# One reordering and one re-layout of an attention, router and mixture-of-experts kernel

## The chip, the cores and the metric

The kernel runs on one core of a Trainium2 chip. The metric is the device time of one execution in microseconds (us). Three executions of the kernel before gave 1012.26, 1013.10 and 1013.12 us; the median is 1013.1 us.

## The reference, cut to what matters

Three stages follow one another. Everything is computed in float32 or better.

```python
# 1. chunked attention: batch 4, 8 heads, 768 positions, head size 64; chunks of 32 queries see
#    16 positions to the left, 8 to the right and 8 memory keys
scores = scale * q_c @ k_full.T ; a = softmax(scores) ; out_c = a @ v_full
x = out as (3072 tokens, 512)
# 2. router and experts: 8 experts, 512 -> 1024 -> 512, one expert for each token
logits = x @ w_gate + modality_bias[modality_id] ; e = argmax(logits)
gate_w = softmax(logits)[e]
y = gate_w * (relu(x @ w1[e]) @ w2[e])
# 3. a rational activation between two products, 512 -> 2048 -> 512
h = y @ w_in
g = (a0 + a1 h + a2 h^2 + a3 h^3) / (1 + |b0 h| + |b1| h^2 + 1e-6)
out = g @ w_out
```

## The kernel before, in words

All instructions are put on their engines' queues in the order of the program text; nothing is reordered by a planner. A framework adds the semaphores. An engine takes its queue in order, so a waiting instruction holds up all behind it on that engine.

**Attention** (lines 30 to 282) works on 24 tiles of 128 tokens in a pipeline. One pass `t` of the loop issues `scores(t)` and `softmax(t)`, the loads of tile t+4, `ptrans(t-1)` (four transposes of the probabilities, copied out by ScalarE), `xtrans(t-3)` (four transposes of the finished values), `exps(t)` and `pv(t-2)` (the product with the values, then sums, reciprocals and a product on VectorE, and the write of the values to DRAM). Every four tiles, `gate1` and `gate2` make router logits. `scores` writes one of the two halves of the PSUM tile `pa` (two banks in one tile), `pv` writes the two banks of `pb`.

**Router in two halves.** Tiles 0 to 15 are routed while attention still runs (`first`, `first_ranks`, then `first_places` in pass 22), which gives two early slots: 128 tokens each of the commonest expert, gathered from DRAM by GpSimd. The weights of that expert are loaded in pass 21. After the loop, the tail of attention (lines 268 to 282) is interleaved with the first products of early slot 0 (`mm1_0(0, kk)`: two float32 matmuls for each kk, which show as four records). `second` (line 519) then routes the other 8 tiles (`pick`, `rank`, `place`, the one-hot products at line 571 that list each slot's tokens), computes both early slots in plain float32 (`mm1_0`, `relu`, `prep_h0`, `mm2_0`), starts slot 2 (`mm1(EARLY, part)`), and makes the gate values: `terms` (a subtraction on VectorE, an exponential on ScalarE), `gates`, `gate_parts`, the wide product `bg` (line 605) and the 24 matmuls at line 616. The outputs of the two early slots and the split of `w2` into a rounded high part and a remainder (`split_hi` on ScalarE, `split_lo` on VectorE) end it.

**Experts** (`moe`, line 827): 24 slots follow. A slot has 24 products `mm1` (line 818) and 24 products `mm2` (line 746), all 128x128 by 128x512 of the rounded type `F32R`, with eight transposes of the hidden values and four of the next slot's tokens between them. `mm1` writes the two banks of `pb`, `mm2` the half `s % 2` of `pa`. A filler converts the third stage's weights beside it. In the last pass four tiles of rows for the third stage are transposed as well (line 863): two into pool tiles, two into the halves of `pb`.

**Third stage** (`moe2`, line 1020): 6 blocks of 512 tokens, each with 16 steps of 12 products `h` (lines 1052 to 1054) and 12 products `a` (lines 1109 to 1111), 2304 in all.

**Where the operands lie.** The allocator rounds each tile up to 32 bytes of a partition. Pools on the left side grow upwards behind the constants, pools on the right side are stacked downwards from the top, and the tiles of one pool follow one another. In the kernel before, the starts modulo 512 bytes are: `ident` 128; `xs`, `hs`, `xg`, `w2h`, `w2l`, `hhl` 416; `w1r`, `w1h`, `w1l`, `w2r` 480 (behind `ys`, 2080 bytes, and `e0`, 32 bytes); early `h0` 384; `wih`, `wil`, `yh`, `yl`, `wo` 192; `gh`, `gl` 256 (behind two tiles `yr` of 2080 bytes).

Of the kernel before, what the change touches and what calls it, by code (L numbers as in the profile page):

```python
# [46 lines left out]
def attention(nc, tc, ex, ident, q, k, v, wg_d, mod, mbias, pos_u, out_u, constants):  # L47
# [8 lines left out]
    with ExitStack() as ctx:  # L56
# [57 lines left out]
        def scores(t):  # L114
            qt, kt = qs[t % NB_IN], kz[t % NB_IN]
            sc = ex.pa[:, t % 2]
            for hp in range(HP):
                for c in range(TC):
                    x = c // 2 * KP + c % 2 * CH
                    nc.tensor.matmul(  # L120
                        sc[CH * c:CH * c + CH, hp * P:hp * P + P], lhsT=qt[:, hp, CH * c:CH * c + CH], rhs=kt[:, :, hp, x:x + 64],
                        start=True, stop=True,
                    )
            sc_t[t] = sc.rearrange("p (h k) -> p h k", k=64)
# [36 lines left out]
        def pv(t):  # L161
            s = pT_t.pop(t)
            w = vz[t % NB_IN]
            ps = ex.pb
            n = 2 * (D + 1)
# [61 lines left out]
        for t in range(NT):  # L227
# [42 lines left out]
        xtrans(NT - 3)  # L270
        ex.prep_x0(0)
        pv(NT - 1)
        ins.close()
        ex.open_w2(ctx)
        xtrans(NT - 2)
        ex.mm1_0(0, 0)
        xtrans(NT - 1)
        gate1(NT // GT - 1, 0, GT - 1)
        ex.mm1_0(0, 1)
        gate2(NT // GT - 1, 0, GT - 1)  # L280
        gate_last(NT - 1)
        rt.second()

# [8 lines left out]
class Router:  # L292
# [226 lines left out]
    def second(self):  # L519
# [3 lines left out]
        for f in self.pick(n, NT):  # L523
            f()
        ex.mm1_0(0, 2)
        ex.split_hi(ex.w1r, ex.w1h, 0)
        ex.mm1_0(0, 3)
        ps = self.rank(n, NT)
        ex.prep_x0(1)
        ex.relu(0)  # L530
        ex.mm1_0(1, 0, 1, 2, 3)
        rest = self.first_rest()
# [11 lines left out]
        for f in (  # L544
# [19 lines left out]
        ):  # L564
            f()
        for i in range(1, 4):
            ex.split_hi(ex.w1r, ex.w1h, i)
        for i in range(2):
            ex.split_lo(ex.w1r, ex.w1h, ex.w1l, i)
        for t in range(NT):  # L570
            nc.tensor.matmul(tb, lhsT=self.at1[:, :, t] if t < n else at2[:, :, t - n], rhs=bt[:, :, t], start=(t == 0), stop=(t == NT - 1))
        ex.prep_h0(0, 0)
        ex.prep_h0(0, 1)
# [9 lines left out]
        V.tensor_scalar(out=f[:, 1], in0=tb, scalar1=0.0, scalar2=-1.0, op0=ALU.is_gt, op1=ALU.mult)  # L583
        ex.relu(1)
        cnt = self.tp.tile([P, 32], F32, tag="t", name="cnt")
        ex.mm2_0(0, 0)
        nc.tensor.matmul(cnt, lhsT=self.ones, rhs=some, start=True, stop=True)
        self.slots(c, end, off, f, cnt)
        for i in range(2, 4):
            ex.split_lo(ex.w1r, ex.w1h, ex.w1l, i)  # L590
# [6 lines left out]
        for part in range(3):  # L597
            ex.mm1(EARLY, part)
            if part < 2:
                ex.prep_h0(1, part)  # L600
        for step in (*rest[2:], *self.terms(n, NT), *self.gates(n, NT), *self.gate_parts()):
            step()
# [18 lines left out]
        V.scalar_tensor_tensor(out=self.ex.gate_s, in0=gs[:, 1], scalar=1.0 / GP, in1=gs[:, 0], op0=ALU.mult, op1=ALU.add)  # L621
        ex.out(0)
        ex.out(1, ex.ys1)
        for i in range(4):
            ex.split_hi(ex.w2r, ex.w2h, i)
            ex.split_lo(ex.w2r, ex.w2h, ex.w2l, i)
        ex.load_w(EARLY, ex.w2r, ex.w2v)

# [27 lines left out]
class Experts:  # L656


    def __init__(self, nc, tc, ident, xd, yd, w1, w2, src_u, pos_u, out_u, gate_s, flags):
        self.nc, self.tc, self.ident = nc, tc, ident  # L660
        self.xd, self.yd, self.src_u, self.pos_u, self.out_u, self.gate_s, self.flags = xd, yd, src_u, pos_u, out_u, gate_s, flags
        self.w1v = w1.rearrange("e (p k) f -> (e p) (k f)", k=4)
        self.w2v = w2.rearrange("e (p j) d -> (e p) (j d)", j=8)
        self.hps, self.yps, self.hT = {}, {}, {}
        self.ctx = ExitStack()
        self.sp = self.ctx.enter_context(tc.tile_pool(name="shared", side="right", bufs=1))
        self.ps = self.ctx.enter_context(tc.tile_pool(name="shared_ps", side="right", bufs=4, space=PSUM))
        self.pa = self.ps.tile([P, 2, 512], F32, name="pa", bufs=1)
        self.pb = self.ps.tile([P, 2, 512], F32, name="pb", bufs=1)
        self.hs = self.sp.tile([P, 8, P], F32, name="hs")  # L670
        self.xs = [self.sp.tile([P, 2, 4, P], F32R, name=f"xs{i}") for i in range(2)]
        self.xg = [self.sp.tile([P, D_M], F32, name=f"xg{i}") for i in range(3)]
        self.ys = self.sp.tile([P, D_M + 1], F32, name="ys")
        self.e0 = self.sp.tile([1, 1], I32, name="e0")
        self.w1r = self.sp.tile([P, 4, 1024], F32, name="w1r")
        self.w1h = self.sp.tile([P, 4, 1024], F32R, name="w1h")
        self.w1l = self.sp.tile([P, 4, 1024], F32R, name="w1l")
        self.w2r = self.sp.tile([P, 4, 1024], F32, name="w2r")
        self.xT = {}
# [61 lines left out]
    def mm2(self, s, g):  # L741
        ps = self.pa[:, s % 2]
        for i, w in ((0, self.w2h), (1, self.w2h), (0, self.w2l)):
# [7 lines left out]
    def out(self, s, y=None):  # L751
        nc, y = self.nc, self.ys if y is None else y
        nc.gpsimd.tensor_copy(y[:, D_M:].bitcast(U32), self.out_u[:, s:s + 1])
        nc.scalar.activation(y[:, 0:D_M], self.pa[:, s % 2], func=AF.Copy, scale=self.gate_s[:, s:s + 1])
        nc.gpsimd.indirect_dma_start(
# [12 lines left out]
    def mm1_0(self, s, *kks):  # L768
        if 0 in kks:
            self.hps[s] = [(self.pa if s == 0 else self.pb)[:, i] for i in range(2)]  # L770
        for kk in kks:
# [12 lines left out]
    def mm2_0(self, s, g):  # L784
        for n in range(4 * g, 4 * g + 4):
            self.nc.tensor.matmul(  # L786
                self.pa[:, s % 2], lhsT=self.h0[g][:, n % 4], rhs=self.w2r[:, n // 2, (n % 2) * 512:(n % 2) * 512 + 512],
                start=(n == 0), stop=(n == 7),
            )
# [19 lines left out]
    def mm1(self, s, part):  # L809
        h, l = self.xT[s]  # L810
        w1h, w1l = self.w1h, self.w1l
        if part == 0:
            self.hps[s] = [(self.pa if s == 0 else self.pb)[:, i] for i in range(2)]
        ps = self.hps[s]
# [12 lines left out]
def moe(nc, tc, ex, filler, rows):  # L827
# [5 lines left out]
    for i in range(EARLY + 1, NM + 1):  # L833
# [27 lines left out]
        if i == NM:  # L861
            for t in range(4):
                ps = ex.ps.tile([P, 4, P], F32, tag="t", name="yps") if t < 2 else ex.pb[:, t - 2].rearrange("p (k n) -> p k n", k=4)
                rows.prep(t, w1r[:, t, 0:D_M + 1], ps, rows.h, rows.l)
# [148 lines left out]
def moe2(nc, tc, rows, wih, wil, wod, consts, out):  # L1013
    with ExitStack() as ctx:
# [145 lines left out]
def program(nc, tc, q, k, v, mod, wg_d, mbias, w1, w2, w_in, w_out, a, b, out):  # L1160
    with tc.manual_schedule(), ExitStack() as ctx:
        cp = ctx.enter_context(tc.tile_pool(name="const", bufs=1))
        dp = ctx.enter_context(tc.tile_pool(name="dram", bufs=1, space=bass.MemoryType.DRAM))
        ident = cp.tile([P, P], F32, name="ident")
        make_identity(nc, ident)
        nc.scalar.preload_act_table_set("natural_log_exp_and_others")
        src_u = cp.tile([P, NS], U32, name="src_u")
        pos_u = cp.tile([P, NS], U32, name="pos_u")
        out_u = cp.tile([P, NS], U32, name="out_u")
# [4 lines left out]
        ex = Experts(nc, tc, ident, xd, yd, w1, w2, src_u, pos_u, out_u, gate_s, flags)  # L1174
        consts = Constants(nc, cp)
# [62 lines left out]
```

## Time and profile before

| what | value |
|---|---|
| runs | 1012.26, 1013.10, 1013.12 us |
| the profiled execution | 1014.01 us, span of its instructions 1012.2 us |
| TensorE matmuls (PE) | 975.7 us busy, 96% of the span |
| TensorE weight loads (PEld) | 780.8 us, 77% |
| VectorE (DVE) | 747.4 us, 74% |
| ScalarE (ACT) | 592.9 us, 59% |
| GpSimd (POOL) | 147.2 us, 15% |
| mean granted TensorE clock | 0.99 of full speed |

Attention takes the first 108 us or so, the second half of the router up to 157 us, the experts up to 463 us, the third stage the rest. A line of the timeline gives the start, the duration, the engine, the source line, what is written from what, the shape, the number of instructions merged into the line, and in brackets how long the engine was idle before it and what ended that. The 1.8 us between span and time lie before and behind the program's own instructions.

### The profile page before, as it was taken

The numbers are of one execution on the slowest core, as the hardware profiler recorded it, in microseconds if no ns is written. First come the engines' busy times: TensorE is split into PE (matmuls) and PEld (weight loads), VectorE is DVE, ScalarE is ACT, GpSimd is POOL, SyncE is SP. The second block draws the span as 40 slices with busy tenths as digits, with TensorE's granted clock in tenths as the row PEclk, the third lists the DMA queues.
The fourth block names the chain that finished last, engine by engine and source line by source line (L and its number), as shares of the span: only waits on it lengthen the run. The fifth ranks groups of instructions, "written<-read, shape, count | busy, mean of one in ns | idle before, by whom it ended". The sixth has DMA issues, their size and how long they took to land.

```text
span 1012.2 us, 16192 instructions
## 1 busy us (share of the span) xinstructions
PE 975.7 (96%) x5809; PEld 780.8 (77%) x5809; DVE 747.4 (74%) x1217; ACT 592.9 (59%) x947; POOL 147.2 (15%) x205
## 2 busy tenths in 40 slices
PE   6998989999999999989999999999999999999997
PEld 4776557888788888867888888888888888888885
DVE  6766555656685553345998988988888888889885
ACT  2543425555575554445766766776667676766673
POOL 5112012111143333220000100100010001001001
PEclk9999999999999999999999999999999999999999
DMA  8999422443696654345130100000010001001001
GB/s 261 377 363 350 178 74 74 123 128 107 203 311 224 234 152 127 114 147 218 65 112 15 42 11 22 31 21 21 22 43 11 22 11 42 21 1 42 1 1 42
DMA packets 37993, 110.43 MB, mean 109 GB/s; under 512 B 6950, under 2 KB 6978, under 8 KB 37892
## 3 DMA queue, kind: packets, MB, share of 16 engines
q1 hardware_dynamic: 27540, 76.43, 22.6%
q0 software_dynamic: 10352, 32.79, 9.2%
q8 instruction: 47, 0.77, 0.3%
q14 instruction: 54, 0.44, 0.1%
HBM read 82.44 MB, written 27.80 MB: 109 GB/s over the span
## 4 chain that ended last, share of the span: by engine, by line
PE 86%; DMA 6%; DVE 3%; issue 3%; ACT 2%; SPq 1%; POOL 0%; POOLq 0%; ACTq 0%; DVEq 0%
PE pb L818 12%; PE pa L746 11%; PE a L1111 9%; PE a L1109 9%; PE a L1110 9%; PE h L1054 8%; PE h L1053 8%; PE h L1052 8%; DMA wod<-wo 2%; PE pb L168 2%; PE pa L120 2%; PE hTp L736 2%; PE pa L786 1%; DMA k<-in_k 1%; PE pps L154 1%
## 5 line engine op out<-in xcount | busy, mean ns | idle before, releaser
L1111 PE MATMUL a<-wo,gl 128*128 128x512 f32 x384 | 152.1, 396 | 1.2 <-DVE gl L1094 1.2
L1109 PE MATMUL a<-wo,gh 128*128 128x512 f32 x384 | 152.0, 396 | 0.6 <-ACT gh L1088 0.6
L1052 PE MATMUL h<-yh,wih 128*128 128x512 f32 x384 | 151.5, 395 | 0.5 <-PEq L876 0.5
L1110 PE MATMUL a<-wo,gh 128*128 128x512 f32 x384 | 151.9, 395 | 0.0
L1054 PE MATMUL h<-yh,wil 128*128 128x512 f32 x384 | 150.0, 391 | 0.0
L1053 PE MATMUL h<-yl,wih 128*128 128x512 f32 x384 | 149.9, 390 | 0.0
L1064 ACT ACTIVATE s<-h 128x512 f32<-128x512 f32 x96 | 56.5, 588 | 84.5 <-PE h L1054 84.5
L818 PE MATMUL pb<-w1h,xs 128*128 128x512 f32 x384 | 101.6, 407 | 2.3 <-ACT w1h L719 2.3
L1071 DVE SCALAR_TENSOR_TENSOR q<-s,absb,q 128x512 f32<-128x512 f32 x96 | 71.8, 748 | 36.2 <-ACT q L1065 35.6
L1111 PEld LDWEIGHTS a<-wo,gl 128*128 128x128 f32 x384 | 72.2, 188 | 19.4 <-DVE gl L1094 2.1
L1088 ACT CAST gh<-u 128x512 fp32r<-128x512 f32 x96 | 59.9, 624 | 46.4 <-DVE u L1084 46.4
L1109 PEld LDWEIGHTS a<-wo,gh 128*128 128x128 f32 x384 | 72.2, 188 | 18.0 <-ACT gh L1088 1.2
L818 PEld LDWEIGHTS pb<-w1h,xs 128*128 128x128 f32 x384 | 71.0, 191 | 18.6 <-ACT w1h L719 2.7
L1110 PEld LDWEIGHTS a<-wo,gh 128*128 128x128 f32 x384 | 72.2, 188 | 17.1
L1052 PEld LDWEIGHTS h<-yh,wih 128*128 128x128 f32 x384 | 72.1, 188 | 15.8 <-issue 0.9
L1054 PEld LDWEIGHTS h<-yh,wil 128*128 128x128 f32 x384 | 72.1, 188 | 15.4
L1053 PEld LDWEIGHTS h<-yl,wih 128*128 128x128 f32 x384 | 72.2, 188 | 15.0
L1066 ACT ACTIVATE u<-h,ab 128x512 f32<-128x512 f32 x96 | 74.9, 780 | 0.0
L1084 DVE SCALAR_TENSOR_TENSOR u<-u,ab,q 128x512 f32<-128x512 f32 x96 | 72.2, 752 | 3.4
L1073 DVE SCALAR_TENSOR_TENSOR u<-u,ab,h 128x512 f32<-128x512 f32 x96 | 71.8, 748 | 3.4
L1082 DVE SCALAR_TENSOR_TENSOR q<-q,cb,s 128x512 f32<-128x512 f32 x96 | 71.8, 748 | 0.1
L1077 ACT ACTIVATE s<-q,cb 128x512 f32<-128x512 f32 x96 | 70.3, 732 | 1.2 <-DVE q L1071 0.2
(227 smaller groups left out, 1729.1 us busy)
## 6 DMA issues: line engine op xcount, KB each, us to landing
v<-in_v SPq DMA_DIRECT2D x48, 260.0 KB
w1r<-in_moe_w SPq DMA_DIRECT2D x16, 512.0 KB
w2r<-in_moe_w SPq DMA_DIRECT2D x16, 512.0 KB
wr<-in_moe_w_in SPq DMA_DIRECT2D x16, 512.0 KB
wr<-in_moe_w_out SPq DMA_DIRECT2D x16, 512.0 KB
wod<-wo POOLq DMA_DIRECT2D x32, 256.0 KB, 2.7
wo<-wod SPq DMA_DIRECT2D x16, 512.0 KB
k<-in_k SPq DMA_DIRECT2D x48, 168.0 KB
```

What stands on the lines that cost most here:

```text
L746: self.nc.tensor.matmul(ps, lhsT=self.hhl[g][i][:, j, :], rhs=w[:, n // 2, (n % 2) * 512:(n % 2) * 512 + 512], start=(i == 0 and w is self ...
L818: self.nc.tensor.matmul(ps[i], lhsT=x[:, kk, :], rhs=w[:, kk, i * 512:(i + 1) * 512], start=(x is h and w is w1h and kk == 0), stop=(w is ...
L1052: nc.tensor.matmul(ps, lhsT=wih[k][:, sl], rhs=h[:, k], start=(k == 0), stop=False)
L1053: nc.tensor.matmul(ps, lhsT=wih[k][:, sl], rhs=l[:, k], start=False, stop=False)
L1054: nc.tensor.matmul(ps, lhsT=wil[k][:, sl], rhs=h[:, k], start=False, stop=(k == NK - 1))
L1066: A.activation(u, ps, func=AF.Identity, scale=a3, bias=a2)
L1071: V.scalar_tensor_tensor(out=q, in0=s, scalar=absb1, in1=q, op0=ALU.mult, op1=ALU.add)
L1073: V.scalar_tensor_tensor(out=u, in0=u, scalar=a1, in1=ps, op0=ALU.add, op1=ALU.mult)
L1084: V.scalar_tensor_tensor(out=u, in0=u, scalar=a0, in1=q, op0=ALU.add, op1=ALU.mult)
L1109: nc.tensor.matmul(ps, lhsT=gh[:, sl], rhs=wo[x][:, 0].bitcast(F32R), start=(x == 0), stop=False)
L1110: nc.tensor.matmul(ps, lhsT=gh[:, sl], rhs=wo[x][:, 1].bitcast(F32R), start=False, stop=False)
L1111: nc.tensor.matmul(ps, lhsT=gl[:, sl], rhs=wo[x][:, 0].bitcast(F32R), start=False, stop=(x == NF - 1))
```

## The change: what it does

1. `pa` and `pb` become lists of two tiles of one bank each. `pv` gets a two-bank tile of its own in attention, whose banks `pb` takes over when attention ends.
2. `first_places` (16 small matmuls and two gathers on GpSimd's queue) moves from pass 22 behind the work of pass 23.
3. In the tail, all logits (`gate1`, `gate2`, `gate_last`) stand ahead of the first early slot's transposes and products.
4. In `second`, `rank` stands ahead of half of `mm1_0(0)`; three quarters of `mm1_0(1)` move behind the one-hot products at line 571; both exponentials (`terms`) come right behind the places instead of behind slot 2's first products; `relu(0)` comes behind them on ScalarE's queue; `relu(1)` and `mm2_0(0, 0)` come behind `slots`, and three of the four `split_lo` of `w1` as well.
5. The four pieces of the `w2` split stand ahead of and between `out(0)` and `out(1)`.
6. Tiles move in SBUF: `ys` and `e0` behind the weights; the constants in another order, `absb1` and `cb` inside `ab`; a pad of 288 bytes ahead of `wih`; `ys1` and `yr` 2560 bytes long in place of 2080. By the same arithmetic as above the new starts modulo 512 are 416 for `ident`, `xs`, `hs`, `xg`, `w1r`, `w1h`, `w1l`, `w2r`, `w2h`, `w2l`, `hhl`, `h0`, `wih`, `wil`, `yh`, `yl`, `wo`, `gh`, `gl` (constants end at 18048, plus 288 is 18336, which is 35 times 512 plus 416). The early slots' `x0` goes from 384 to 320.

```diff
-            sc = ex.pa[:, t % 2]
+            sc = ex.pa[t % 2]
...
-            ps = ex.pb
+            ps = ex.pv
...
             if t == G3 + 3:
                 chore(len(chores))
+            if t == NT - 1:
                 rt.first_places()
...
         xtrans(NT - 3)
-        ex.prep_x0(0)
         pv(NT - 1)
         ins.close()
         ex.open_w2(ctx)
         xtrans(NT - 2)
-        ex.mm1_0(0, 0)
+        gate1(NT // GT - 1, 0, GT - 1)
         xtrans(NT - 1)
-        gate1(NT // GT - 1, 0, GT - 1)
-        ex.mm1_0(0, 1)
         gate2(NT // GT - 1, 0, GT - 1)
         gate_last(NT - 1)
+        ex.prep_x0(0)
+        ex.mm1_0(0, 0, 1)
         rt.second()
...
         for f in self.pick(n, NT):
             f()
-        ex.mm1_0(0, 2)
+        ps = self.rank(n, NT)
+        ex.mm1_0(0, 2, 3)
         ex.split_hi(ex.w1r, ex.w1h, 0)
-        ex.mm1_0(0, 3)
-        ps = self.rank(n, NT)
         ex.prep_x0(1)
-        ex.relu(0)
-        ex.mm1_0(1, 0, 1, 2, 3)
+        ex.mm1_0(1, 0)
...
+        terms, last = rest[2:4], self.terms(n, NT)
+        terms[0]()
+        last[0]()
+        terms[1]()
+        last[1]()
+        ex.relu(0)
         for i in range(1, 4):
             ex.split_hi(ex.w1r, ex.w1h, i)
-        for i in range(2):
-            ex.split_lo(ex.w1r, ex.w1h, ex.w1l, i)
+        ex.split_lo(ex.w1r, ex.w1h, ex.w1l, 0)
         for t in range(NT):
             nc.tensor.matmul(tb, ...)
+        ex.mm1_0(1, 1, 2, 3)
...
-        ex.relu(1)
         cnt = self.tp.tile([P, 32], F32, tag="t", name="cnt")
-        ex.mm2_0(0, 0)
         nc.tensor.matmul(cnt, lhsT=self.ones, rhs=some, start=True, stop=True)
         self.slots(c, end, off, f, cnt)
-        for i in range(2, 4):
+        ex.relu(1)
+        ex.mm2_0(0, 0)
+        for i in range(1, 4):
             ex.split_lo(ex.w1r, ex.w1h, ex.w1l, i)
...
-        for step in (*rest[2:], *self.terms(n, NT), *self.gates(n, NT), *self.gate_parts()):
+        for step in (*rest[4:], *self.gates(n, NT), *self.gate_parts()):
...
-        ex.out(0)
-        ex.out(1, ex.ys1)
-        for i in range(4):
+        for i in range(2):
             ex.split_hi(ex.w2r, ex.w2h, i)
             ex.split_lo(ex.w2r, ex.w2h, ex.w2l, i)
+        ex.out(0)
+        for i in range(2, 4):
+            ex.split_hi(ex.w2r, ex.w2h, i)
+            ex.split_lo(ex.w2r, ex.w2h, ex.w2l, i)
+        ex.out(1, ex.ys1)
...
-        self.pa = self.ps.tile([P, 2, 512], F32, name="pa", bufs=1)
-        self.pb = self.ps.tile([P, 2, 512], F32, name="pb", bufs=1)
+        self.pa = [self.ps.tile([P, 512], F32, name=f"pa{i}", bufs=1) for i in range(2)]
+        self.pvx = ExitStack()
+        self.pv = self.pvx.enter_context(...).tile([P, 2, 512], F32, name="pv")
...
-        self.ys = self.sp.tile([P, D_M + 1], F32, name="ys")
-        self.e0 = self.sp.tile([1, 1], I32, name="e0")
         self.w1r = self.sp.tile([P, 4, 1024], F32, name="w1r")
...
+        self.ys = self.sp.tile([P, D_M + 1], F32, name="ys")
+        self.e0 = self.sp.tile([1, 1], I32, name="e0")
...
-        self.ys1 = p.tile([P, D_M + 1], F32, name="ys1")
+        self.ys1 = p.tile([P, D_M + 128], F32, name="ys1")[:, 0:D_M + 1]
...
-                ps = ... if t < 2 else ex.pb[:, t - 2].rearrange(...)
+                ps = ... if t < 2 else ex.pb[t - 2].rearrange(...)
...
-        self.ab = cp.tile([P, 6], F32, name="ab")
-        self.absb1 = cp.tile([P, 1], F32, name="absb1")
-        self.cb = cp.tile([P, 1], F32, name="cb")
+        self.ab = cp.tile([P, 8], F32, name="ab")
+        self.absb1, self.cb = self.ab[:, 6:7], self.ab[:, 7:8]
...
-            yr[blk, t] = rp.tile([P, DM + 1], F32, tag="yr", name="yr")
+            yr[blk, t] = rp.tile([P, DM + 128], F32, tag="yr", name="yr")[:, 0:DM + 1]
...
+        wp.tile([P, 72], F32, name="pad")
```

## Rows read from the trace of the kernel before

**Rows 1.** The page: busy time of each engine; TensorE in 40 slices.

```profile
PE 975.7 (96%) x5809; PEld 780.8 (77%) x5809; DVE 747.4 (74%) x1217; ACT 592.9 (59%) x947; POOL 147.2 (15%) x205
PE   6998989999999999989999999999999999999997
```

**Rows 2.** Timeline of the stretch in which the first places wait.

```profile
93.01 1.09 PE L168 MATMUL pb<-v,pT 128*32 128x130 f32 x32
...
96.77 1.16 PE L514 MATMUL tb<-bt,at 128*128 128x2 f16 x16 [2.67 <-DVE bt L495]
...
98.97 1.09 POOL L697 DMA_INDIRECT xg<-xd,src_u  x1 [1.71 <-DVE src_u L515]
...
104.02 0.66 PE L154 MATMUL pps<-ident,pt 128*128 128x128 f32 x4 [0.57 <-ACT pt L145]
...
106.66 0.67 PE L765 MATMUL xps<-ident,xg 128*128 128x128 f32 x4
```

**Rows 3.** Windows: stretch, busy by engine (x instructions), clock, DMA share, GB/s.

```profile
98.00:100.00 2.00, 2.00 (x34) 1.52 (x32) 0.13 (x1) 0.00 (x0) 1.03 (x1) 0.50 0.95 346
```

**Rows 4.** Chain of waits, a full-clock pass of attention: start, duration, what.

```profile
62.62 1.08 PE pa L120 x32
63.71 0.59 PE pps L154 x4
64.29 0.99 PE gps L199 x8
...
69.46 0.44 PE xps L191 x4
```

**Rows 5.** Timeline: the gate values and the matmuls that wait for them.

```profile
143.04 0.29 DVE L444 TENSOR_REDUCE route<-logits 128x16 f32<-128x128 f32 x1 [5.58 <-ACT logits L402]
...
146.03 4.20 DVE L605 TENSOR_TENSOR bg<-be,g 128x2304 f16<-128x2304 f16 x1
...
150.28 1.69 PE L616 MATMUL gp<-bg,at 128*128 128x96 f16 x24 [2.42 <-DVE bg L605]
...
157.21 1.27 ACT L754 ACTIVATE ys<-pa,gate_s 128x512 f32<-128x512 f32 x2 [4.96 <-PE pa L786]
```

**Rows 6.** Chain of waits: `mm2_0` before and behind that wait.

```profile
134.12 3.44 PE pa L786 x8
...
151.97 5.20 PE pa L786 x8
```

**Rows 7.** Timeline: a copy of ScalarE in the tail of attention.

```profile
107.36 0.59 ACT L766 COPY x<-xps 128x512 f32<-128x512 f32 x1
```

**Rows 8.** Timeline: the end of the experts.

```profile
449.24 0.60 PE L936 MATMUL pb<-ident,w1r 128*128 128x128 f32 x4
...
452.06 1.29 DVE L939 TENSOR_TENSOR yl<-yps,yh 128x512 fp32r<-128x512 f32 x2 [1.16 <-DMA wod<-wo]
...
454.00 1.11 PE L936 MATMUL pb<-ident,w1r 128*128 128x128 f32 x4 [4.16 <-DVE yl L939]
...
454.77 2.06 PE L746 MATMUL pa<-w2h,hh 128*128 128x512 f32 x4
...
459.62 1.07 PE L746 MATMUL pa<-w2h,hh 128*128 128x512 f32 x4
```

**Rows 9.** Waits in attention, 20 to 95 us: us in total, times, longest us.

```profile
PE pa L120 <- DVE rs L174: 1.0, 3, 0.4
```

**Rows 10.** Timeline of the third stage, single matmuls.

```profile
599.77 0.39 PE L1053 MATMUL h<-yl,wih 128*128 128x512 f32 x1
...
602.27 0.40 PE L1109 MATMUL a<-wo,gh 128*128 128x512 f32 x1
...
607.64 0.39 PE L1111 MATMUL a<-wo,gl 128*128 128x512 f32 x1
```

**Rows 11.** Chain of waits: one slot of the experts.

```profile
176.50 5.49 PE pa L746 x24
181.98 1.86 PE pb L818 x8
```

More of the change, by code (lines that the diff above doesn't have):

```diff
@@ L667, in __init__ @@
         self.ps = self.ctx.enter_context(tc.tile_pool(name="shared_ps", side="right", bufs=4, space=PSUM))
-        self.pa = self.ps.tile([P, 2, 512], F32, name="pa", bufs=1)
-        self.pb = self.ps.tile([P, 2, 512], F32, name="pb", bufs=1)
+        self.pa = [self.ps.tile([P, 512], F32, name=f"pa{i}", bufs=1) for i in range(2)]
+        self.pvx = ExitStack()
+        self.pv = self.pvx.enter_context(tc.tile_pool(name="a_pv", side="right", bufs=1, space=PSUM)).tile([P, 2, 512], F32, name="pv")
         self.hs = self.sp.tile([P, 8, P], F32, name="hs")
@@ L678, in __init__ @@
         self.w2r = self.sp.tile([P, 4, 1024], F32, name="w2r")
+        self.ys = self.sp.tile([P, D_M + 1], F32, name="ys")
+        self.e0 = self.sp.tile([1, 1], I32, name="e0")
         self.xT = {}
     def open_w2(self, ctx):
+        self.pvx.close()
+        p = self.ctx.enter_context(self.tc.tile_pool(name="shared_h", reuse_waits="tile", side="right", bufs=1, space=PSUM))
+        self.pb = [p.tile([P, 512], F32, name=f"pb{i}") for i in range(2)]
         p = self.ctx.enter_context(self.tc.tile_pool(name="shared_w2", reuse_waits="tile", side="right", bufs=1))
@@ L741, in mm2 @@
     def mm2(self, s, g):
-        ps = self.pa[:, s % 2]
+        ps = self.pa[s % 2]
         for i, w in ((0, self.w2h), (1, self.w2h), (0, self.w2l)):
@@ L753, in out @@
         nc.gpsimd.tensor_copy(y[:, D_M:].bitcast(U32), self.out_u[:, s:s + 1])
-        nc.scalar.activation(y[:, 0:D_M], self.pa[:, s % 2], func=AF.Copy, scale=self.gate_s[:, s:s + 1])
+        nc.scalar.activation(y[:, 0:D_M], self.pa[s % 2], func=AF.Copy, scale=self.gate_s[:, s:s + 1])
         nc.gpsimd.indirect_dma_start(
@@ L769, in mm1_0 @@
         if 0 in kks:
-            self.hps[s] = [(self.pa if s == 0 else self.pb)[:, i] for i in range(2)]
+            self.hps[s] = self.pa if s == 0 else self.pb
         for kk in kks:
@@ L786, in mm2_0 @@
             self.nc.tensor.matmul(
-                self.pa[:, s % 2], lhsT=self.h0[g][:, n % 4], rhs=self.w2r[:, n // 2, (n % 2) * 512:(n % 2) * 512 + 512],
+                self.pa[s % 2], lhsT=self.h0[g][:, n % 4], rhs=self.w2r[:, n // 2, (n % 2) * 512:(n % 2) * 512 + 512],
                 start=(n == 0), stop=(n == 7),
@@ L812, in mm1 @@
         if part == 0:
-            self.hps[s] = [(self.pa if s == 0 else self.pb)[:, i] for i in range(2)]
+            self.hps[s] = self.pa if s == 0 else self.pb
         ps = self.hps[s]
@@ L862, in moe @@
             for t in range(4):
-                ps = ex.ps.tile([P, 4, P], F32, tag="t", name="yps") if t < 2 else ex.pb[:, t - 2].rearrange("p (k n) -> p k n", k=4)
+                ps = ex.ps.tile([P, 4, P], F32, tag="t", name="yps") if t < 2 else ex.pb[t - 2].rearrange("p (k n) -> p k n", k=4)
                 rows.prep(t, w1r[:, t, 0:D_M + 1], ps, rows.h, rows.l)
@@ L1163, in program @@
         dp = ctx.enter_context(tc.tile_pool(name="dram", bufs=1, space=bass.MemoryType.DRAM))
+        src_u = cp.tile([P, NS], U32, name="src_u")
+        pos_u = cp.tile([P, NS], U32, name="pos_u")
+        consts = Constants(nc, cp)
         ident = cp.tile([P, P], F32, name="ident")
@@ L1166, in program @@
         nc.scalar.preload_act_table_set("natural_log_exp_and_others")
-        src_u = cp.tile([P, NS], U32, name="src_u")
-        pos_u = cp.tile([P, NS], U32, name="pos_u")
         out_u = cp.tile([P, NS], U32, name="out_u")
@@ L1174, in program @@
         ex = Experts(nc, tc, ident, xd, yd, w1, w2, src_u, pos_u, out_u, gate_s, flags)
-        consts = Constants(nc, cp)
         attention(nc, tc, ex, ident, q, k, v, wg_d, mod, mbias, pos_u, out_u, lambda: consts.load(a, b))
```

## The prediction

> **What bounds the kernel now.** First the page's busy shares: TensorE is busy 96% of the span, VectorE 74%, ScalarE 59% [rows 1]. So TensorE sets the time nearly everywhere, and a change can gain in two ways alone: fill a hole in TensorE's row, or make its instructions closer together. The 40 slices show where the holes are: outside the filling of the pipeline, the digits fall to 8 in the slices that hold 76 to 101, 127 to 152 and 455 to 480 us [rows 1]. Next the brackets in TensorE's timeline, for what it waited for in them: 2.67 us at 96.8, 2.42 at 150.3 and 4.16 at 454.0 are the waits that the change touches [rows 2, 5, 8]. Last, single rows of the timeline, for the distance between matmuls that wait for nothing [rows 10, 11].
>
> **Part A, router and early slots (94 to 157 us).** What is lost there today:
> - TensorE ends a value product at 93.01 + 1.09 = 94.10 and stands until 96.77, since the 16 place matmuls are queued ahead of tile 23's scores and wait for VectorE's one-hot [rows 2]: 2.67 us.
> - [...] From 96.77 to 104.02 pass 7.25 us for work that takes 1.16 + 1.08 + 0.59 + 0.99 + 0.44 + 1.09 = 5.35 us at full clock [rows 2, 4]: 1.90 us.
> - The gate matmuls wait 2.42 us for `bg`; the products behind them take 5.20 in place of 3.44 us, at the lower clock again [rows 5, 6]: 2.42 + 1.76 = 4.18 us.
>
> Together 8.75 us. After the change tile 23's scores follow the product at 94.1 at once, and the places come when their one-hot has long been made. The exponentials no longer stand behind ScalarE's copies of slot 1's hidden values (VectorE is idle 5.58 us before the sums at 143.04, for the exponential [rows 5]); they run near 118 us. VectorE then has behind `slots` three remainders of `w1`, slot 2's remainder and the eleven small steps, which took 146.03 - 143.04 = 3.0 us with the waits in them [rows 5]; by my reckoning of its queue `bg` starts near 136 and ends 4.20 us later, near 140, while TensorE reaches the gate matmuls near 146. So the wait goes and has 5 us to spare; late next is nothing on that path.
>
> What is added: the logits used to be covered by `mm1_0(0)`, and now stand bare. TensorE waits for the copy of tile 22's values (0.59 us, and 0.06 to signal), for the rest of the logits' copy (0.15, as transposes lie over most of it), for tile 23's copy behind it (about 0.3), and for `x0` (0.65), each sized from the one copy of 0.59 us [rows 7]; and `prep_x0(0)` no longer fills the place where tile 23's product waits for VectorE (0.5 with the like). Sum 2.25 us. Net gain 8.75 - 2.25 = 6.5 us; bounds: 8.75 with no new wait at all, 2 if the gathers land late (below).
>
> Moved past queues: on GpSimd the first gather leaves at 98.97 now and is read at 106.66, 7.7 us later [rows 2]; it will leave about 1.7 us later and be read near 107.8, so it keeps some 7 us. On SyncE nothing changes its order. On ScalarE `relu(0)` waits for the exponentials, and so for VectorE's places, about 1.5 us longer; queued behind it are three roundings of `w1` and the copies of the hidden values, but TensorE works on 12 records of `mm1_0(1)` meanwhile: nothing. The three `w1` remainders behind `slots` end near 132, their readers start near 139: nothing. `out(0)` and the `w2` split: `out(0)` reads only half 0 of `pa`, yet waits 4.96 us until the last product into half 1 [rows 5]. This shows that halves of one tile hold each other up; with one bank each it runs earlier, beside TensorE's work: nothing by itself, only slack.
>
> **Part B, the last expert pass.** The same false dependence, on the path: the fourth transpose group writes half 1 of `pb` and waits 4.16 us until VectorE has read half 0, and starts at 454.00 [rows 8]. With two tiles it follows the third at once, at 449.7, and the last `mm2` starts near 450.15 in place of 454.77: 4.6 us. Behind the hole `mm2` is also slow: twelve products take 459.62 - 454.77 = 4.85 us [rows 8], against 12 x 5.49 / 24 = 2.75 in a slot without a hole [rows 11]: 2.1 us more. Sum 6.7 us. Late next would be VectorE's last remainder (four steps of 1.29 / 2 us from 452.06: near 454.7), ahead of the end of `mm2` at about 455.7: hidden. If it were not, 1 us is lost. Elsewhere the halves cost little: in attention `scores` waits 1.0 us in all for VectorE [rows 9], but the DMA share is about 1 there as in the window shown [rows 3], so I count 0 and keep 1 for the range.
>
> **Part C, distances between matmuls.** In the third stage eleven `h` products take 602.27 - 599.77 = 2.50 us, 227.3 ns each; 23 `a` products take 607.64 - 602.27 = 5.37 us, 233.5 ns each [rows 10]. Same shape, type and clock. In the experts `mm2` has 5.49 / 24 = 228.8 ns, `mm1` 1.86 / 8 = 232.5 ns [rows 11]. Set beside the starts of the operands modulo 512, the two quick kinds have both operands at one start (192/192, 416/416), the two slow ones 64 bytes apart (256/192, 416/480). I take it that the difference decides. After the change all four are at 416/416, like today's `mm2`. Gain: 1152 `a` products x 6.2 ns = 7.1 us by the rows, taken as 6.4 since `h` loses a little behind transposes; 24 x 24 = 576 `mm1` products x 3.7 ns = 2.1 us. VectorE does not become the bound: its 74% leaves room for 1%. Bounds: 0 and 10 us. The plain float32 products, `x0` included, run at half that rate and I give them nothing.
>
> [...]
>
> **Sum.** 6.5 + 6.7 + 6.4 + 2.1 = 21.7 us off the profiled execution's 1014.0: 992.3. That execution is 0.9 us above the median of the runs, so 991.4, written 991.5.
>
> **Rivals.**
> - The placement does nothing (bank order or the kind of product sets the distance): A and B alone, 991.5 + 8.5 = 1000.0. For it: four kinds of products are few, and they differ in more than placement. Against: the split is clean.
> - Part A is given back: `prep_x0(0)` waits for its gather, all logits' products being past, with `rank` queued behind it on TensorE. For it: DMA is nearly full then (0.95) [rows 3]. Against: no wait today at 7.7 us from issue to use [rows 2]. 991.5 + 6.5 = 998.
> - Part B turns into another wait (the remainders wait for the store of the converted weights that frees their tile): 991.5 + 6.7 = 998.2. Against: that wait is over at 452.06 [rows 8].
> - Slower: 416 is 32 past a multiple of 64, and `h` leaves 192 for it. If the start itself costs, all 2304 third-stage products pay. It decides the sign from 13.2 us / 2304 = 5.7 ns each above today's mean of 230.4; with one more step of 6.2 ns on the slow kind, 239.7 ns, it is 2304 x 9.3 = 21.4 us: 1014.0 - 13.2 + 21.4 - 0.9 = 1021.3. Against: `mm2` at 416/416 is among the quick [rows 11].
>
> **How the numbers follow.** Forecast 0.62, placement without effect 0.17, A given back 0.10, B another wait 0.08, slower 0.03. The forecast's own spread is 986.5 (A with no new wait, C at 10, attention's 1) to 996; to reach the rivals the range goes to 1000.5. Within 0.2% (2 us, about what a measurement tells from no change) would need most of A, B and C to fail together: 0.02, taken from the first three rivals. Faster 0.95, slower 0.03.
>
> **What would show it.** Right: no wait of TensorE above 1 us near 97, 150 and 454 us; a granted clock of 1.0 in those stretches; `a` and `mm1` at 227 to 229 ns; slot 3's `mm1` starting near 150; the third stage's first product near 448. Wrong: `a` still at 233 ns; a wait at the early slot's transposes; `h` slower than 228 ns; VectorE late for `bg`.

## The result and the profile after

The changed kernel takes 997.48 us (median of five runs, 995.18 to 999.25) against 1013.12 of the kernel before: 0.985 of its time (0.983 to 0.986). The forecast was 991.5, in a range of 986.5 to 1000.5. Its profiled execution is also 997.48 us long, 16.5 less than the profiled one of before. By TensorE's rows (first and last product of each part):

| stretch | before | after | gain | predicted |
|---|---|---|---|---|
| start to slot 3's `mm1` | 156.61 | 151.39 | 5.2 | 6.5 |
| slot 3's `mm1` to the last `mm2` | 305.5 | 297.7 | 7.8 | 6.7 + 2.1 |
| last `mm2` to first `h` | 0.9 | 3.9 | -3.0 | 0 |
| third stage, first to last product | 542.8 | 536.2 | 6.6 | 6.4 |

Part A, timeline of TensorE (start, duration, line and operation; in brackets idle time before it and what ended it):

```profile
96.62 0.72 PE L514 MATMUL tb<-bt,at 128*128 128x2 f16 x9
98.75 0.54 PE L514 MATMUL tb<-bt,at 128*128 128x2 f16 x7 [1.41 <-issue]
...
104.46 0.85 PE L199 MATMUL gps<-xT,wg 128*32 128x384 f32 x8 [0.68 <-ACT xT L192]
...
108.88 5.33 PE L784 MATMUL pa<-w1r,x 128*128 128x512 f32 x8 [0.67 <-ACT x L777]
...
146.81 1.64 PE L620 MATMUL gp<-bg,at 128*128 128x96 f16 x24
148.29 3.67 PE L797 MATMUL pa<-w2r,h 128*128 128x512 f32 x8
151.39 0.79 PE L829 MATMUL pb<-w1h,xs 128*128 128x512 f32 x1
```

The wait for the one-hot [rows 2] and the one for `bg` [rows 5] are gone, and the products behind the gate take 3.67 us, at a granted clock of 1.00 from 148 to 152 us. In the kernel before the same view has 5.36 (the chain of [rows 6] gives 5.20), at a clock of 0.50 from 152 to 154 us and 0.67 from 154 to 156:

```profile
151.81 5.36 PE L786 MATMUL pa<-w2r,h 128*128 128x512 f32 x8
```

New are a hole of 1.41 us in the middle of the places, which no engine releases and which none of the ten later traces of the new order has, and eight `mm1_0` products that take 5.33 us (the next eight take 3.68): the windows show the lower clock there (columns as in [rows 3]).

```profile
108.00:110.00 2.00, 1.33 (x4) 0.62 (x4) 1.74 (x9) 1.53 (x2) 0.00 (x0) 0.69 1.03 398
110.00:112.00 2.00, 2.00 (x4) 0.91 (x3) 0.00 (x0) 0.00 (x0) 0.00 (x0) 0.50 0.59 223
```

Part B, the same view at the end of the experts:

```profile
442.98 1.04 PE L947 MATMUL pb<-ident,w1r 128*128 128x128 f32 x8
...
448.44 1.07 PE L757 MATMUL pa<-w2l,hh 128*128 128x512 f32 x4
453.00 0.47 PE L1062 MATMUL h<-yh,wih 128*128 128x512 f32 x1 [3.50 <-PEq L887]
453.31 0.44 PE L1063 MATMUL h<-yl,wih 128*128 128x512 f32 x1
453.55 0.63 PE L1064 MATMUL h<-yh,wil 128*128 128x512 f32 x1
```

The transposes that waited 4.16 us [rows 8] now wait for nothing, and the last products run at full clock (1.00 from 444 to 450 us). But the third stage starts 3.50 us late: line 887 is the branch around the overflow slots, and PEq is TensorE's own sequencer. Behind it the products take 0.63 in place of 0.39 us until the clock is back:

```profile
454.00:456.00 2.00, 2.00 (x6) 1.61 (x5) 0.00 (x0) 0.00 (x0) 0.00 (x0) 0.50 0.86 211
456.00:458.00 2.00, 2.00 (x8) 1.54 (x8) 0.00 (x0) 0.32 (x1) 0.00 (x0) 0.77 0.95 315
```

Part C: the mean distance between starts of `a` products is 226.8 ns (before 233.3), of `h` products 227.3 (228.1).

### The profile page after: what moved, and what is told of

Read it like the earlier page. It is cut to its first block, busy times and chain, and to the rows that moved or that the text cites. A ratio compares the mean times of both kernels' runs of the same rounds, so it can differ in the third digit from the quotient of the medians.

```text
span 995.7 us, 16192 instructions
## 1 busy us (share of the span) xinstructions
PE 962.3 (97%) x5809; PEld 780.6 (78%) x5809; DVE 747.8 (75%) x1217; ACT 593.6 (60%) x947; POOL 147.4 (15%) x205
## 4 chain that ended last, share of the span: by engine, by line
PE 64%; DMA 2%; issue 1%; DVE 1%; ACT 0%; POOL 0%; POOLq 0%; SPq 0%; ACTq 0%
PE a L1121 9%; PE a L1119 9%; PE a L1120 8%; PE h L1064 8%; PE h L1062 8%; PE h L1063 8%; PE pa L757 6%; PE pb L829 6%; DMA wod<-wo 2%; PE hTp L747 1%; PE yps L947 1%; DMA yr<-yd 1%; PE xps L814 0%; DVE gl L1104 0%; DVE u L1094 0%
## 5 line engine op out<-in xcount | busy, mean ns | idle before, releaser
L1121 PE MATMUL a<-wo,gl 128*128 128x512 f32 x384 | 149.8, 390 | 1.3 <-DVE gl L1104 1.3
L1119 PE MATMUL a<-wo,gh 128*128 128x512 f32 x384 | 149.7, 390 | 0.7 <-ACT gh L1098 0.7
L1120 PE MATMUL a<-wo,gh 128*128 128x512 f32 x384 | 149.6, 390 | 0.0
L1081 DVE SCALAR_TENSOR_TENSOR q<-s,ab,q 128x512 f32<-128x512 f32 x96 | 71.8, 747 | 32.0 <-ACT q L1075 32.0
L1092 DVE SCALAR_TENSOR_TENSOR q<-q,ab,s 128x512 f32<-128x512 f32 x96 | 71.7, 747 | 0.1
L1087 ACT ACTIVATE s<-q,ab 128x512 f32<-128x512 f32 x96 | 70.2, 731 | 1.3
```

The lines of the kernel that those rows point to most:

```text
L1081: V.scalar_tensor_tensor(out=q, in0=s, scalar=absb1, in1=q, op0=ALU.mult, op1=ALU.add)
L1092: V.scalar_tensor_tensor(out=q, in0=q, scalar=cb, in1=s, op0=ALU.add, op1=ALU.mult)
L1119: nc.tensor.matmul(ps, lhsT=gh[:, sl], rhs=wo[x][:, 0].bitcast(F32R), start=(x == 0), stop=False)
L1120: nc.tensor.matmul(ps, lhsT=gh[:, sl], rhs=wo[x][:, 1].bitcast(F32R), start=False, stop=False)
L1121: nc.tensor.matmul(ps, lhsT=gl[:, sl], rhs=wo[x][:, 0].bitcast(F32R), start=False, stop=(x == NF - 1))
```

## The experiments

Ratios are to the kernel before on the same chip, with the 95% interval. The experiments lay on three chips: `e1` to `e4` on one, `after_again` and `e5` to `e9` on the second, `e10` and `e11` on the third; the chip of the first measurement isn't on record.

**The wait at the branch.** The line's own events, by engine, in the changed kernel (count, durations min/median/max in ns, first and last start):

```profile
L887 PEldq EVENT_SEMAPHORE  x2: 51/51/51, 449.7 to 452.7; - x2
L887 ACTq EVENT_SEMAPHORE  x2: 17/17/17, 452.5 to 452.6; - x2
...
L887 PEldq COMPARE_BRANCH  x1: 3618/3618/3618, 446.0 to 446.0; - x1
```

TensorE's branch takes 3.6 us, nearly all of it beside its own products; that was so before the change too (3.3 us, and a wait of 0.52). But here the two small steps behind it lie 3.1 us apart (0.2 before the change). Between them the DMA view of 450 to 452 us lists a fetch of code (queue, packets, MB, share):

```profile
q8 instruction: 1, 0.02, 3.7%
```

And in the kernel before:

```profile
463.02 0.47 PE L1052 MATMUL h<-yh,wih 128*128 128x512 f32 x1 [0.52 <-PEq L876]
```

Theory, the author's inference from the fetch between the two steps: the branch's target is the last instruction of a fetched block. Rival: TensorE waits for another engine there, ScalarE say, whose steps lie just ahead (452.5). `e1_shift` makes its program 16 instructions longer ahead of the branch:

```diff
-        nc.tensor.matmul(cnt, lhsT=self.ones, rhs=some, start=True, stop=True)
+        for _ in range(9):
+            nc.tensor.matmul(cnt, lhsT=self.ones, rhs=some, start=True, stop=True)
```

> The changed kernel, with one small matmul (ones by the slot flags, 32 columns) issued nine times in place of once, near 130 us: 16 more instructions (8 weight loads, 8 matmuls) in TensorE's program ahead of the branch, nothing else. In the changed kernel the third stage's first product comes at 453.00, 3.5 us after the last expert product, and the trace names the branch as releaser. Theory 'code block': the branch's target is the last instruction of a 16 KB block of TensorE's program, and the next block is fetched (450.25 to 451.44) only when the first is used up. 16 instructions later the target lies inside a block, so the wait falls below 0.6 us, the granted clock behind it stays at 1.0 (now 0.50 in 454 to 456), and the run takes 997.5 - 3.0 - 1.7 + 0.4 for the added matmuls = 993.2 us. Rival 'join': TensorE waits there for ScalarE or GpSimd, which pass the same branch at 449.94 and 451.70; then the shift does nothing, the wait stays at 3.5 us and the run takes 997.9.

Measured: 997.02 us, 0.983 (0.981 to 0.985), beside 0.991 of the changed kernel run again (below). The wait is 0.56 us and the third stage takes 534.7 in place of 536.2 us, so the lower clock cost 1.6 (unrounded):

```profile
457.06 0.47 PE L1063 MATMUL h<-yh,wih 128*128 128x512 f32 x1 [0.56 <-PEq L888]
457.36 0.39 PE L1064 MATMUL h<-yl,wih 128*128 128x512 f32 x1
```

Nothing but the length of the program changed, and the wait fell from 3.50 to 0.56 us, as the code theory has it; that a block ends just there is not shown by itself. That the time missed 993.2 comes from the router, where this run's slot 3 starts at 158.2 (below).

**Part B alone**, `e4_banks`: the kernel before with `pa` and `pb` as lists of single banks and attention's value product in its own pool.

> The kernel before, with part B alone: the accumulators of the experts as single banks, and attention's value product in a pool of its own; order and placement as before. Theory 'false dependence': the wait of 4.16 us of the fourth transpose group goes and the last products run at full clock, 6.7 us, so 1013.1 - 6.7 = 1006.4 us if the code behind the branch is there in time, and about 1009.4 to 1011.1 if it is 3 us late and the clock falls too. The wait at the branch is read for itself. Rival: single banks do nothing by themselves, the wait stays, 1013.1.

Measured: 1010.22 us, 0.997 (0.995 to 0.998). Slot 3 to the last `mm2` takes 299.0 us against 305.5: 6.5 for the predicted 6.7. Then both small steps and one product come through, and the second product waits:

```profile
454.36 0.47 PE L1056 MATMUL h<-yh,wih 128*128 128x512 f32 x1 [0.75 <-PEq L880]
457.11 0.39 PE L1057 MATMUL h<-yl,wih 128*128 128x512 f32 x1 [2.28 <-issue]
```

This fits the code theory. Ahead of the branch TensorE's trace has 120 wait steps here and 125 in the changed kernel, and the stall comes five records later here (two wait steps, two weight loads and a product). All seven traces with 125 steps stall between the two small steps, both with 120 (`e4_banks`, `e9_order_before`) behind the first product; the kernel before, with 141, and the four kernels with 16 more instructions don't stall (waits of 0.52 us, and of 0.6 to 0.8 in the four). So the single banks themselves, with fewer wait steps, give back behind the branch about 2.5 of the 6.5 us (0.75 and 2.28 in place of 0.52); that they bring the branch target near a block's end is the author's reading.

**Part C.** Three kernels change one start each: the tiles ahead of `gh` and `gl` 32 bytes smaller (`e2_diff64`) or larger (`e5_diff_other`), and no pad (`e3_start128`).

```diff
-  yr[blk, t] = rp.tile([P, DM + 128], F32, tag="yr", name="yr")[:, 0:DM + 1]
+  yr[blk, t] = rp.tile([P, DM + 120], F32, ...)   # e2: 352/416;  DM + 136 in e5: 480/416
-  wp.tile([P, 72], F32, name="pad")               # e3: removed, 128/128
```

> The changed kernel, with the two tiles ahead of the third stage's gate values 32 bytes smaller each: the stationary operand of the a products then starts at 352 modulo 512, the moving one stays at 416; 64 bytes apart, as before the change (256 and 192). All else is unchanged. Theory 'difference': the a products go back from 226.7 to 233.3 ns, 1152 x 6.6 = 7.6 us, so 997.5 + 7.6 = 1005.1 us, and the h products stay at 227.3 ns. Rival 'something else of the change' (single banks, other starts): a stays at 226.7 ns and the run at 997.5.

> The changed kernel, with the two tiles ahead of the third stage's gate values 32 bytes larger each: the stationary operand of the a products starts at 480 modulo 512, the moving one stays at 416; 64 bytes apart in the other direction than in the experiment with 352 and 416, and in the direction of the kernel before (256 and 192). With 352 and 416 an a product took 229.0 ns, against 226.8 at 416 and 416 and 233.3 before. Theory 'signed difference': stationary ahead of moving by 64 costs 6.5 ns, behind it by 64 costs 2.2 ns; so 233.3 ns here, third stage 1145 x 6.5 = 7.4 us longer, 1005 us. Rival 'the pair of starts decides, not the difference': another value, anywhere from 226.8 to 235.

> The changed kernel without the pad ahead of the third stage's weights: every operand of the third stage then starts at 128 modulo 512 in place of 416, stationary and moving alike. Theory 'difference': the difference is still 0, so both kinds of product stay at 227 ns and the run at 997.5 us. Rival 'the start itself': 416 is 32 bytes past a multiple of 64, 128 is a multiple of it; if that counts, both kinds change, by 1 ns or more each, 2304 x 1 = 2.3 us or more, either way.

| stationary/moving start | `a`, ns | third stage, us | ratio |
|---|---|---|---|
| 416/416 (run again) | 226.8 | 536.2 | 0.991 (0.988 to 0.993) |
| 128/128, e3 | 226.9 | 536.3 | 0.991 (0.989 to 0.992) |
| 352/416, e2 | 229.0 | 538.4 | 0.990 (0.988 to 0.993) |
| 480/416, e5 | 233.4 | 544.2 | 0.996 (0.994 to 0.998) |

In e5's timeline 24 `a` products start from 598.24 to 603.60: 5.36 / 23 = 233 ns; in e2's 18 from 595.73 to 599.62: 3.89 / 17 = 229 ns.

```profile
598.24 0.40 PE L1119 MATMUL a<-wo,gh 128*128 128x512 f32 x1
...
603.60 0.40 PE L1121 MATMUL a<-wo,gl 128*128 128x512 f32 x1
```

```profile
595.73 0.39 PE L1119 MATMUL a<-wo,gh 128*128 128x512 f32 x1
...
599.62 0.39 PE L1121 MATMUL a<-wo,gl 128*128 128x512 f32 x1
```

For the `a` products the common start does nothing, the difference decides, with its sign: the stationary operand 64 bytes ahead costs 6.6 ns, 64 behind 2.2. The first expectation (233.3 for e2) missed the sign. The whole runs, 1002.90 us (e2), 1004.02 (e3) and 1009.08 (e5), missed what was expected of them, two by 4 us and more, mainly because the router's part varies by several us (below); so the stage is compared, not the run.

In the experts the gain came otherwise than foreseen. `mm1` in one slot, before and then after:

```profile
181.82 2.02 PE L818 MATMUL pb<-w1h,xs 128*128 128x512 f32 x8
183.68 0.60 PE L736 MATMUL hTp<-ident,hs 128*128 128x128 f32 x4
184.03 2.11 PE L818 MATMUL pb<-w1h,xs 128*128 128x512 f32 x8
185.98 0.60 PE L736 MATMUL hTp<-ident,hs 128*128 128x128 f32 x4
...
194.23 2.02 PE L818 MATMUL pb<-w1h,xs 128*128 128x512 f32 x8
```

```profile
176.52 1.98 PE L829 MATMUL pb<-w1h,xs 128*128 128x512 f32 x8
178.34 0.60 PE L747 MATMUL hTp<-ident,hs 128*128 128x128 f32 x4
178.69 2.10 PE L829 MATMUL pb<-w1h,xs 128*128 128x512 f32 x8
180.63 0.60 PE L747 MATMUL hTp<-ident,hs 128*128 128x128 f32 x4
...
188.86 1.98 PE L829 MATMUL pb<-w1h,xs 128*128 128x512 f32 x8
```

From start to start of these groups, the first eight products of a slot take 1.82 us in place of 1.86, some 5 ns less each; the eight behind the transposes take 1.94 in place of 1.95, next to nothing less, and the last eight 1.94 both times. A slot takes 12.34 us in place of 12.41: over 24 slots about 1.7 us.

**Part A measured again.** `after_again` is the changed kernel unchanged, `e6_terms_late` puts its exponentials back, `e9_order_before` is the change without part A (old order, with banks and placement).

```diff
-        terms, last = rest[2:4], self.terms(n, NT)     # e6: these five go,
-        terms[0](); last[0](); terms[1](); last[1]()
-        for step in (*rest[4:], *self.gates(n, NT), *self.gate_parts()):
+        for step in (*rest[2:], *self.terms(n, NT), *self.gates(n, NT), *self.gate_parts()):
```

> The changed kernel itself once more, beside the next three on one chip, since the first four runs of experiments lay on a chip whose runs of the kernel before spread from 1011 to 1017 us. Expected if the ground is the same: 997.5 us, with the wait of 3.5 us at the branch. In the traces of the first experiments one signal of TensorE near 101 us came 2.4 us late (not so in the first trace of the changed kernel); if that goes with the chip, it shows here too.

> The changed kernel, with the exponentials of the gates (two subtractions and two activations) put back to where they stood before, behind the early slots' hidden values; the rest of the new order stays. Theory of the prediction: the exponentials decide when the gate values are ready, so the wait of the gate products for bg comes back (2.4 us before) and the products behind it run at the lower clock (1.8 us): slot 3's mm1 4 us later than in the changed kernel, 997.5 + 4.2 = 1001.7 us. Rival: the wait went because the rest of the router runs earlier now, and the place of the exponentials does nothing: 997.5.

> The kernel before with the single banks and the placement of the change, and the whole old order of the router and the early slots: the change without part A. Theory of the prediction, with what the first trace showed: part A is worth 5.2 us (slot 3's products at 151.4 in place of 156.6), so this takes 997.5 + 5.2 = 1002.7 us beside a changed kernel of 997.5. Rival: on the chips of these experiments the changed order loses 2.5 us to the late signals and more to the clock behind them (a changed kernel of 1004.2), and the old order loses as much or nothing; then part A is worth nothing there, and this takes the same time as the changed kernel, 1002 to 1005. The wait at the branch is read for itself.

Measured: 1004.24, 0.991 (0.988 to 0.993), runs 998.11 to 1004.80; 1008.23, 0.994 (0.992 to 0.997); 1000.72, 0.988 (0.986 to 0.989). The exponentials do what was predicted: the wait for `bg` is back at 2.41 us, the products behind it take 5.07 us, slot 3's `mm1` comes at 161.58 against 156.87. But the whole of part A is worth nothing here: with the old order slot 3 starts at 157.13, with the new one at 156.87. By medians the old order is even 3.5 us quicker, but the two intervals meet, and 1.0 us of it is a shorter stall at the branch (0.65 and 2.21 us in place of 3.86):

```profile
157.13 2.41 PE L822 MATMUL pb<-w1h,xs 128*128 128x512 f32 x8
...
455.54 0.47 PE L1055 MATMUL h<-yh,wih 128*128 128x512 f32 x1 [0.65 <-PEq L880]
458.22 0.48 PE L1056 MATMUL h<-yl,wih 128*128 128x512 f32 x1 [2.21 <-issue]
```

In `after_again` slot 3 starts 5.5 later than in the first trace; tile 23's value product waits:

```profile
99.30 1.09 PE L168 MATMUL pv<-v,pT 128*32 128x130 f32 x32
...
103.93 0.32 PE L168 MATMUL pv<-v,pT 128*32 128x130 f32 x4 [2.51 <-ACT xT L192]
```

```profile
102.70 0.17 DVE L174 TENSOR_SCALAR rs<-pv 128x8 f32<-128x8 f32 x1 [3.62 <-PE xps L191]
```

```profile
99.92 1.10 POOL L708 DMA_INDIRECT xg<-xd,src_u  x1 [3.17 <-DVE src_u L515]
101.32 1.02 POOL L708 DMA_INDIRECT xg<-xd,src_u  x1 [0.30 <-issue]
```

Tile 22's value product ends by 100.39, yet VectorE, which needs it alone, starts at 102.70, 0.36 us after GpSimd has issued the second gather; ScalarE's copy of tile 21's values, whose transposes end by 101.42, starts at 102 us or later (the windows have one instruction of 0.59 us for it in 102 to 104), in the first trace of the change 0.04 us after its transposes. Of the eight traces of the new order with both gathers in a row, seven have the wait of tile 23's value product, 2.5 to 2.6 us, and the first one of the change doesn't (0.28). In the old order both gathers stand in a row as well, and there the signals needn't be late: in `e4_banks` ScalarE's copy starts 0.09 us after its transposes end, in the middle of the second gather, and in `e9_order_before` 0.10 us after, during the first; only in the kernel before it starts 1.03 us after.

```profile
98.65 1.12 PE L154 MATMUL pps<-ident,pt 128*128 128x128 f32 x4
99.50 1.02 POOL L701 DMA_INDIRECT xg<-xd,src_u  x1 [0.30 <-issue]
99.86 0.59 ACT L156 COPY pT<-pps 128x512 f32<-128x512 f32 x1 [5.74 <-PE pps L154]
```

In `after_again` the clock falls behind it: 0.60, 0.50 and 0.50 in the three stretches of 4 us from 104 to 116.

**The gathers.** `e8_gather_split` (on top of `e7_x0_early`, below) and `e10_split_only` (on the change) issue the second gather behind the last logits:

```diff
-        for s in range(EARLY):
-            self.ex.gather(s)
+        self.ex.gather(0)     # row 1 is kept in a small tile; gather(1) follows gate_last
```

> The last kernel (code 16 instructions later, slot inputs transposed early), with the second of the two early gathers issued by GpSimd some 10 us later, behind the last logits, in place of right behind the first. In seven of the eight traces of the changed order, TensorE's signals of three groups near 101 us come 1.3 to 2.4 us late, all within 0.12 us, and 0.3 to 0.45 us after GpSimd ends the issue of the second gather; tile 23's value product waits 2.5 us for it and the clock falls behind it. Theory 'gathers hold the signals': the hold now ends 0.3 to 0.45 us after the first gather's issue, 1.4 us earlier, so the wait falls from 2.5 to 1.1 us or less and the run gains 1.3 us and up to 2 us of clock: 989 to 990.5 against 991.8. Rival 'something else of that moment': the wait stays at 2.5 us and the run at 991.8.

> The changed kernel with one edit: the second early gather is issued behind the last logits in place of right behind the first. Slot inputs and code length stay as in the change. Theory 'two gathers in a row hold TensorE's signals': the wait of tile 23's value product (2.5 us in the second trace of the changed kernel) goes, as it went in the run with split gathers; with it goes part of the lower clock behind it, so slot 3's mm1 starts 3 to 5 us earlier than the 156.9 of that trace, and the run takes 1004.2 - 2.5 - 1 to 2 = 999.5 to 1000.7 us, against 1000.7 for the old order with the same banks and placement. Rival 'chance': the hold was absent in that run as it was in the first trace of the change; then it is here again, and the run takes 1004.

Measured: 995.95, 0.983 (0.981 to 0.985), and 996.18, 0.983 (0.980 to 0.985). In both the wait is 0.27 us, and in the third kernel with split gathers (below) 0.36:

```profile
102.33 1.09 PE L168 MATMUL pv<-v,pT 128*32 128x130 f32 x32 [0.27 <-issue]
```

The clock in the same stretches of `e10_split_only` is 1.00, 0.67 and 0.90, and slot 3 starts at 151.77. The expected hold behind the first gather alone (1.1 us) isn't there, so in the new order the second gather right behind the first matters; by which mechanism, and what else it takes, stays open. A rival isn't excluded for two of the three: they lie on a chip on which no kernel with both gathers in a row was traced; on the chip of `e8_gather_split` all four traces of the new order with both in a row show the hold (2.5 to 2.6 us). `e10_split_only` gains more than expected, 8 us by medians against the changed kernel run again, which lay on another of the three chips. `e8_gather_split` was expected at 989 to 990.5 and was slower than its parent (0.979); 1.6 us of that is in its trace: without the hold the early transposes come before their gather has landed.

```profile
108.51 1.10 PE L785 MATMUL xps<-ident,xg 128*128 128x128 f32 x4 [1.59 <-DMA xg<-xd,src_u]
```

The parent's traced execution, with the hold, took 995.92 us and its other four 990.55 to 992.76; whether those had the hold, no trace tells.

**A faster version.** `e7_x0_early` has the longer program and both slot inputs transposed earlier; `e11_best` the longer program, split gathers, and slot 1's input alone earlier.

```diff
-        ex.mm1_0(0, 2, 3)
+        ex.mm1_0(0, 2)
         ex.split_hi(ex.w1r, ex.w1h, 0)
         ex.prep_x0(1)
+        ex.mm1_0(0, 3)
```

> The changed kernel with three edits that the traces point to: the 16 more instructions ahead of the branch (wait at the branch 0.6 in place of 3.5 us); the transposes of slot 0's input ahead of the last logits, so that its copy lies beside them and not bare (0.67 us); the transposes of slot 1's input one product pair earlier, for the same reason (0.67 us). Theory: 997.5 - 4.7 + 0.4 - 0.9 - 0.67 = 991.6 us. Rival 'the gather is late': slot 0's input is not there 1.4 us earlier, TensorE waits for it with the last logits queued behind, and the rank after them: no gain from the second edit, or a loss to 2 us, 993 to 995.

> The changed kernel with the gathers split, 16 more instructions ahead of the branch, and slot 1's input transposed one product pair earlier; slot 0's transposes stay behind the last logits, since they waited 1.6 us for their gather when they stood ahead of them. Theory: against the run with the same edits and the early transposes (995.4 in its trace) the 1.6 us go and a copy of 0.67 us stands bare again: 994.5; the clock behind the logits may give 1 more. Rival: the clock falls anyway at the light stretch of 103 to 109 us, and it stays at 995 to 996, no better than the kernel with both gathers in a row and early transposes (991.8).

Measured: 991.78, 0.979 (0.977 to 0.981), and 990.90, 0.977 (0.975 to 0.979). Both beat the change; the intervals of the two overlap. In `e11_best`:

```profile
448.41 1.07 PE L766 MATMUL pa<-w2l,hh 128*128 128x512 f32 x4
450.15 0.47 PE L1071 MATMUL h<-yh,wih 128*128 128x512 f32 x1 [0.68 <-PEq L896]
```

## Why the prediction was right, and where it was not

The direction came out, and the time lies 6 us above the forecast, inside the range. That it lies inside is partly luck: the same kernel run again (`after_again`) took 1004.24 us, beyond the range's 1000.5, and five of its six runs 1003.02 or more. Of the prediction's own signs, the spacing of `a` and `h` and the gate values in time came true; no wait above 1 us (1.41 and 3.50), a full clock in those stretches (0.50 from 454 to 456), all of `mm1` at 227 to 229 ns, and the third stage near 448 (453.00) did not.

Two of TensorE's waits in part A after the change, and one from before:

```profile
102.11 1.09 PE L168 MATMUL pv<-v,pT 128*32 128x130 f32 x32 [0.28 <-issue]
...
119.18 1.98 PE L784 MATMUL pb<-w1r,x 128*128 128x512 f32 x4 [0.67 <-ACT x L777]
```

```profile
120.00 7.13 PE L773 MATMUL pb<-w1r,x 128*128 128x512 f32 x16 [0.68 <-ACT x L766]
```

- **Part A**, 6.5 predicted, 5.2 in the first trace. Of these, 1.5 lie ahead of 94 us, where part A hasn't begun: the product of [rows 2] at 93.01 stands at 91.51. In the other traces it stands anywhere from 91.30 to 95.57, so that is the chance of one execution, and part A itself gave 3.7. The three losses of the old order went as worked out, 8.75 us (of the 1.90 put down to the clock, which is 0.50 in [rows 3], 0.57 was a wait for ScalarE [rows 2]). The new waits are 0.28, 0.68 and 0.67, in sum 1.63 for 2.25; the wait for slot 1's input (0.67) was there before (0.68). Not foreseen: the hole in the places (1.41) and the slow clock of `mm1_0` (5.33 - 3.68 = 1.65). That leaves 8.75 - 1.63 - 3.06 = 4.1 for the measured 3.7; the rest isn't settled. In the later traces the rival "part A is given back" came true in amount, not by its mechanism: the gather was in time, but two gathers in a row went with late signals.
- **Part B**, the false dependence: 6.5 for 6.7, shown alone. The step that failed is "late next would be VectorE's last remainder ... hidden". Late next was TensorE's program itself: the wait behind the branch is 3.50 us in place of 0.52, with a fetch of 0.02 MB of code in it, 3.0 us more, and 1.6 of slow clock; that the branch's target had moved to the end of a code block is the author's theory. The branch's own 3.6 us stayed hidden, as before the change. Of the 5.2 us that the profiled execution lies above the sum (992.3), this is 4.6; what part A fell short and the third stage gave more nearly cancel. The rival that part B turns into another wait named the size nearly (998.2) and the wrong wait.
- **Part C**, third stage: 536.2 with 1.6 of slow clock, 534.7 without: 8.1 us for 6.4; I had rounded 7.1 down and left out `h` (0.9). In the experts 1.6 by `e9_order_before` against `e4_banks` (297.4 against 299.0), for 2.1, but not as foreseen: only eight of a slot's 24 `mm1` products came closer, by 5 ns, where 3.7 was taken for all. "The difference decides" is shown for `a`; the start 416 as a cost is excluded (226.8 ns at 416/416, 226.9 at 128/128). The prediction took a distance of 64 bytes to cost the same either way; in `a` the direction that `mm1` had (stationary behind) costs 2.2 ns, so a size doesn't carry over from one kind of product to another. That placement does nothing is excluded for `a`: e5 and the run again, with all else equal, differ by 8.0 us in the third stage.
- The stall that moves with the number of instructions ahead bears the code theory out. The fetch of 0.02 MB (48 packets of that queue make 0.79 MB in the whole profile, 16 KB each) stands in the stall, but the kernel before has one in 462 to 464 us too, with a wait of 0.52; the size of a block in instructions no run shows. The prediction would have gained by weighing what the change does to the branch, which stands in the trace before.

## What to carry to other kernels

When a change alters how many instructions lie ahead of a branch, read the wait behind the branch again: here it grew from 0.52 to 3.50 us, 4.6 us with the slow clock behind it, and 16 more instructions brought it to 0.56. Try one start modulo 512 for both operands of a product (that 512 is the period, no run tests), and see in the trace which products gain: here `a` went from 233.3 to 226.8 ns, and only eight of a slot's 24 `mm1` gained, 5 ns each. Judge a change of order by traces of several executions and chips: here one of eight missed a wait of 2.5 us that the others have.

## What the runs showed of the hardware

- A wait of TensorE that the profile puts down to its own sequencer went with the length of its program: 3.50 us behind the branch, 0.56 with 16 instructions more.
- Stationary minus moving start, modulo 512: 0 gives 226.8 ns, -64 gives 229.0, +64 gives 233.4 for the `a` products (128x512, F32R); `mm1` products behind transposes gained nothing from going to 0 (1.94 us for eight, 1.95 before).
- In the new order, two gathers in a row went with signals of TensorE up to 2.4 us late in seven of eight traces; with one gather, in none of three (waits of 0.27 to 0.36 us). In the old order two in a row went without late signals in two of three traces.
